# Other places and other lead for some loads of a retention-and-two-MLPs kernel: raw w_out, the joint products' weights, kept sums, activations

## The chip, the cores and the metric

The kernel runs on one core of one Trainium2 chip. The metric is device time in microseconds (us) of that core, from runs of the whole program; a second view is one profiled execution with its trace. Engines are called as in the profile: PE (matmuls), PEld (weight loads), DVE (vector), ACT (scalar), POOL, SP (a queue that here only issues DMAs).

## What is computed

Attention with a decay (no softmax) over 8 batches, 8 heads, 576 positions, head width 64; its output, 4608 tokens by 512, goes through two MLPs, 512 to 2048 to 512 each:

```python
ret = scores * Dmat[None]            # scores = q k^T / 8, Dmat = gamma**(i-j), lower triangle
x = matmul(ret, v)                   # -> 4608 x 512
h = x @ moe_w_in;   x = (h * sigmoid(1.702 * h)) @ moe_w_out
h = x @ moe2_w_in;  y = (h - tanh(h)) @ moe2_w_out
```

All of it is float32 to the outside. A product in the kernel is three passes over split operands (a high part rounded to fp32r and the remainder), `PASS` in the code.

## The kernel before

Tokens are cut into 9 blocks of 512, the inner dimension 2048 into 16 slices of 128. A "step" `n` of the first MLP is one slice of one block: `mm_in` (12 matmuls into one PSUM bank, L614), then `act_a` (a tanh on ACT, L628, and one operation on DVE, L630). Sixteen steps make a visit of a block. DVE and ACT run their instructions in the order in which the program gives them, and so does SP: a DMA whose buffer is not free yet holds up all DMAs behind it on SP. `h` has four PSUM banks, so PE can be some steps ahead of DVE.

**The sums.** The second product of the first MLP is done for visits 5 to 8 in pairs, by seven products of sums of quarters (a Winograd form) instead of eight. The operands of these products are formed while visits 6 and 8 run (`SUMMED`). Each odd step of such a visit calls `sums(u)` (L1206): two activations of this visit (`a21`, `a22`) and two of the visit before, which `firsts_load` (L1192) brought back from DRAM, give five results in four DVE operations (L1215 to L1218). The results go to DRAM by `stores` (L1180), named s1, s2 (in a place of `room`), s3 (the buffer of a21), s4 (the buffer of the loaded a12) and a22. `firsts_load` has three places, taken in turn, so a load for `u` waits for the store of s4 of `u - 3`.

**Raw w_out.** The weights of the same products are formed by `t_prep` (L964), a generator that is advanced by one piece per step: load two raw slices of w_out (tile `wr`, L990), two pairs of subtractions (L985), two splits into high part and remainder in `room` (L980, L981), two stores (`wt`, L971). Its tiles were the two of tag `gl`, so a pair is loaded one step ahead of its first subtraction.

**The joint products.** While the second MLP's first products run (`mm_part`, 6 matmuls each, L1042), the generator `out_units` is advanced in between; in its steps `k` of the joint kind a step is 12 matmuls (`mm_joint`, L741) on four accumulators: two pairs of blocks by two halves of the columns. There are seven stages of eight steps (`STAGES`). At the end of a stage each accumulator is emptied by `evac_joint` (L761); in five stages DVE adds a sum kept in DRAM (L774), which `kept_load` (L746) fetches at the start of the step with `q == 6`, that is one step ahead of the last. Two of the four tiles for it come from the rotation of six that `act_2` (L634) uses for its results (`turn("t")`). The step's weights come by `wj_load` (L276), in pairs, two steps ahead of the first; its activations by `g_load` (L702) into four places in turn, from which `act_b` (L713) splits them (L716 on ACT, L717 on DVE). Next to these, `wq_load` (L1005) fetches the second MLP's weights, two DMAs of 1 MB and 0.75 MB per `u`, and `g_store` (L655) stores its activations.

**The change of stages.** At step 141 of the first MLP (`n == NB * NF - 3`) the first weights and activations of the direct products of blocks 3 onward are loaded (`w_ahead`, `g_ahead`), and the first activation is split in the same step.

Of the kernel before, what the change touches and what calls it, by code (L numbers as in the profile page):

```python
# [8 lines left out]
F32 = mybir.dt.float32  # L9
# [8 lines left out]
P = 128  # L18
# [36 lines left out]
def kernel(  # L55
# [189 lines left out]
    def joint(k):  # L245
        return N1 <= k < N1 + NJ
# [25 lines left out]
        nc.sync.dma_start(out=t.rearrange("p a n -> p (a n)").bitcast(F32), in_=wo_d[int(j >= NB), f])  # L272

    wj = {}

    def wj_load(i):  # L276

        t = place(2 + i // 2 % 2)
        for n in range(2):
            stage, q = divmod(i + n, NF // 2)  # L280
            what, at_, h = STAGES[stage][1]
            src = wo_d[0, q + at_] if what == "o" else wt_d[q]
            c = ((0 if what == "o" else 2 * at_) + h) * DM
            nc.sync.dma_start(out=t[:, n].bitcast(F32), in_=src[:, c:c + DM])
            wj[i + n] = t[:, n].rearrange("p (a c) -> p a c", a=2)

    def wo_stay(f):

# [368 lines left out]
        nc.sync.dma_start(out=gd[s], in_=tt.pop(s))  # L657

    second = {}
    turns = {"t": 0, "gl": 0}  # L660

    def turn(what):

        shape, dt, n = {"t": ([P, BLK], F32, 3), "gl": ([P, BLK], F32, 2)}[what]
        i = turns[what]
        turns[what] += 1
        more = {"t": 3, "gl": 2}[what]
        if second and i % (n + more) >= n:
            return second["pool"].tile(shape, dt, tag=what + "2", name=what, bufs=more)
        return t_p.tile(shape, dt, tag=what, name=what, bufs=n)  # L670
# [12 lines left out]
    def joint_item(x):  # L683
        return N1 <= x < N1 + 2 * NJ
# [13 lines left out]
        return place(spot)  # L698

    def g_load(x):  # L700
        gl[x] = turn("gl")
        o = item(x)  # L702
        if joint_item(x):
            i, r = o
            stage, q = divmod(i, NF // 2)
            name = STAGES[stage][0]
            ja = ORDER[JOINT[r]]
            src = gd[ja * NF + q + (NF // 2 if name == "a12" else 0)] if name in ("a11", "a12") else gs[ja, name, q]
        else:
            src = gd.pop(step_of(o))  # L710
        nc.sync.dma_start(out=gl[x], in_=src)
# [34 lines left out]
    def kept_load(k):  # L746

        stage, q = divmod(k - N1, NF // 2)
        name = STAGES[stage][3]
        if name is None or q != NF // 2 - 2:  # L750
            return
        for y in range(4):
            r, m = divmod(y, 2)
            if y < 2:
                t = second["pool"].tile([P, BLK], F32, tag="o", name="kept", bufs=3)
            else:
                t = turn("t")
            nc.sync.dma_start(out=t, in_=kept_d[name, r, m])
            kept_t[y] = t
# [73 lines left out]
    def w_ahead(k):  # L833

        if not second:
            while n_w[0] <= min(k + 2, DIRECT * NF - 1):
                wo_load(n_w[0])
                n_w[0] += 1
            return
        if k == N1 - 2:  # L840
            wj_load(0)
        if joint(k) and (k - N1) % 2 == 0 and k + 2 < N1 + NJ:
            wj_load(k + 2 - N1)
        while n_w[0] <= min(k + 3, n_steps - 1):
            if joint(n_w[0]):
                n_w[0] = N1 + NJ
            elif n_w[0] == N1 + NJ and k < N1 + NJ - 2:
                break
            else:
                wo_load(n_w[0])  # L850
                n_w[0] += 1

    def g_ahead(x):

        while second and n_g[0] <= min(x + (7 if joint_item(x) else 4), n_b[0] + 3, n_items - 1):
            g_load(n_g[0])
            n_g[0] += 1
        while second and n_b[0] < n_items:
# [105 lines left out]
    def t_prep():  # L964
# [18 lines left out]

        h = slice(0, DM // 2), slice(DM // 2, DM)
        sub = lambda o, a, b: nc.vector.tensor_tensor(out=o, in0=a, in1=b, op=ALU.subtract)  # L985
        for q in range(NF // 2):
            wt_d[q] = dram.tile([P, 4 * DM], F32, tag=f"wt{q}", name="wt")
            lo, hi = ts = [t_p.tile([P, DM], F32, tag="gl", name="wr", bufs=2) for _ in range(2)]
            for i in range(2):
                nc.sync.dma_start(out=ts[i], in_=r_d[q + i * NF // 2])  # L990
            yield
            store()
            sub(lo[:, h[0]], lo[:, h[1]], lo[:, h[0]])
            sub(lo[:, h[1]], hi[:, h[1]], lo[:, h[1]])
            yield
# [3 lines left out]
            yield  # L999
            store()  # L1000
            halves_of(1, hi)
            yield
            store()

# [75 lines left out]
    def x2_std():  # L1080
        t = x_p.tile([P, KD, BLK], F32, tag="x", name="x2s")
        nc.sync.dma_start(out=t, in_=x2_d[0])
        yield
        xo["std"] = []
        for k in range(KD):
            xo["std"].append(xo_tile())
# [119 lines left out]
    def sums(u):  # L1206
# [9 lines left out]
        nc.vector.tensor_tensor(out=s2, in0=s1, in1=a11, op=ALU.subtract)  # L1216
        nc.vector.tensor_tensor(out=a12, in0=a12, in1=s2, op=ALU.subtract)
        nc.vector.tensor_tensor(out=a21, in0=a11, in1=a21, op=ALU.subtract)  # L1218
        done.extend(((j - 1, n, q), t) for n, t in (("a22", a22), ("s1", s1), ("s2", s2), ("s4", a12), ("s3", a21)))

    def some(it, n):
        for _ in range(n):
# [9 lines left out]
    for n in range(LAG, NB * NF):  # L1232
# [17 lines left out]
        if j in SUMMED:  # L1250
            u = SUMMED.index(j) * NF // 2 + f // 2
            if f % 2:
                sums(u)
                stores(5)
                if f < NF - 4:
                    firsts_load(u + 2)
            else:
                stores(2)
        else:
            if n >= LAG + DIRECT * NF:  # L1260
                done.append(s)
# [8 lines left out]
            spare = [x_p.tile([P, 2, 2, DM], F32R, tag="y", name="spare", bufs=2) for _ in range(2)]  # L1270
            room += [spare[i][:, k] for k in range(2) for i in range(2)]
        some(prep, 1)
        if n == NB * NF - 3:
            w_ahead(DIRECT * NF - 2)
            g_ahead(DIRECT * NF - 2)
        if j == NB - 1 and f >= 5:
            some(std, 1)
        if j == NB - 1 and f == 8:
            wq_load(0, True)
# [182 lines left out]
```

## Time and profile before

| | |
|---|---|
| median of 3 runs | 1758.8 us (1753.51 to 1760.52) |
| the profiled execution, its own time | 1754.56 us |
| its span, first to last instruction | 1752.8 us |
| mean granted PE clock | 0.980 |
| PE busy | 1663.6 us, 95% |
| DVE busy | 1225.8 us, 70% |
| ACT busy | 885.5 us, 51% |
| DMA moved | 510.6 MB, mean 291 GB/s |

PE is busy for 95% of the span, so the time is PE's work, plus the stretches in which PE waits, plus what PE loses where it is granted the half clock (0.50 in the tables below). The trace can be asked for who waited for whom, for the order of an engine's instructions in time, and for busy times by stretch. "DMA share" is the mean busy share of the 16 DMA engines.

### The profile page before, as it was taken

The numbers are of one execution on the slowest core, as the hardware profiler recorded it, in microseconds if no ns is written. First come the engines' busy times: TensorE is split into PE (matmuls) and PEld (weight loads), VectorE is DVE, ScalarE is ACT, GpSimd is POOL, SyncE is SP. The second block draws the span as 40 slices with busy tenths as digits, with TensorE's granted clock in tenths as the row PEclk, the third lists the DMA queues.
The fourth block names the chain that finished last, engine by engine and source line by source line (L and its number), as shares of the span: only waits on it lengthen the run. The fifth ranks groups of instructions, "written<-read, shape, count | busy, mean of one in ns | idle before, by whom it ended". The sixth has DMA issues, their size and how long they took to land.

```text
span 1752.8 us, 25320 instructions
## 1 busy us (share of the span) xinstructions
PE 1663.6 (95%) x8874; PEld 1348.8 (77%) x8874; DVE 1225.8 (70%) x1958; ACT 885.5 (51%) x1633; POOL 109.4 (6%) x99
## 2 busy tenths in 40 slices
PE   7999999999999698799999788889999999999999
PEld 5787888887888586588887666678888888888887
DVE  6787877878866657367687777666877777677542
ACT  5443443344432232356577566555776667666542
POOL 2111101221232000000000000000000000000000
PEclk8999999999999899899999899999999999999999
DMA  9566779889998878998898888889999988888962
GB/s 277 177 216 219 256 244 324 299 288 320 345 322 301 300 251 307 327 339 305 309 327 295 265 306 270 288 309 349 313 316 340 326 307 316 312 301 311 372 215 87
DMA packets 195504, 510.60 MB, mean 291 GB/s; under 512 B 21809, under 2 KB 31153, under 8 KB 186417
## 3 DMA queue, kind: packets, MB, share of 16 engines
q1 hardware_dynamic: 182704, 486.88, 80.0%
q10 hardware_dynamic: 12672, 22.11, 3.4%
q8 instruction: 70, 1.15, 0.3%
q14 instruction: 58, 0.47, 0.1%
HBM read 361.05 MB, written 147.85 MB: 290 GB/s over the span
## 4 chain that ended last, share of the span: by engine, by line
PE 70%; DMA 14%; DVE 9%; ACT 3%; issue 3%; SPq 2%; ACTq 0%; POOL 0%; DVEq 0%
PE acc L804 22%; PE h L614 13%; PE acc L800 12%; PE x L1042 8%; PE y L1042 4%; PE h L1029 2%; PE acc L741 2%; DMA gl<-gd 2%; PE w L1042 2%; DMA gl<-gs 2%; DMA wos<-wd 1%; DMA wr<-wr 1%; DVE t L630 1%; PE pat L536 1%; DMA gs<-t 1%
## 5 line engine op out<-in xcount | busy, mean ns | idle before, releaser
L614 PE MATMUL h<-xh,wi 128*128 128x512 f32 x1152 | 377.9, 398 | 22.9 <-DVE t L630 22.1
L804 PE MATMUL acc<-wos,g 128*128 128x512 f32 x1344 | 329.8, 390 | 5.3 <-DVE kept L774 5.3
L716 ACT ACTIVATE g<-gl 128x512 fp32r<-128x512 f32 x244 | 152.1, 628 | 304.0 <-PE acc L804 160.0
L804 PEld LDWEIGHTS acc<-wos,g 128*128 128x128 f32 x1344 | 252.9, 188 | 58.3 <-DVE kept L774 5.7
L717 DVE TENSOR_TENSOR g<-gl,g 128x512 fp32r<-128x512 f32 x244 | 166.6, 687 | 169.0 <-ACT g L716 167.4
L614 PEld LDWEIGHTS h<-xh,wi 128*128 128x128 f32 x1152 | 219.4, 190 | 76.8 <-DVE t L630 27.0
L614 PE MATMUL h<-xl,wi 128*128 128x512 f32 x576 | 227.4, 395 | 0.4 <-DVE xl L443 0.4
L1042 PE MATMUL x<-xo,wq 128*128 128x512 f32 x768 | 196.9, 392 | 0.0
L800 PE MATMUL acc<-g,wos 128*128 128x512 f32 x768 | 186.5, 392 | 1.4 <-DMA wos<-wd 1.1
L1042 PEld LDWEIGHTS x<-xo,wq 128*128 128x128 f32 x768 | 146.0, 190 | 30.9
L800 PEld LDWEIGHTS acc<-g,wos 128*128 128x128 f32 x768 | 142.8, 188 | 33.8 <-issue 2.7
L131 ACT ACTIVATE e<-e,ebias 128x512 int32<-128x512 int32 x64 | 46.4, 725 | 204.6 <-DVE e L129 199.2
L630 DVE SCALAR_TENSOR_TENSOR t<-t,h 128x512 f32<-128x512 f32 x144 | 97.5, 682 | 49.5 <-ACT t L628 49.4
L651 DVE SCALAR_TENSOR_TENSOR pl<-pl,sq 128x512 f32<-128x512 f32 x144 | 99.5, 691 | 42.3 <-ACT pl L648 40.2
L614 PEld LDWEIGHTS h<-xl,wi 128*128 128x128 f32 x576 | 109.8, 191 | 23.1 <-DVE xl L443 1.1
L741 PE MATMUL acc<-g,wos 128*128 128x512 f32 x408 | 106.1, 399 | 18.4 <-DVE kept L774 10.3
L653 DVE COPY_PREDICATED t<-marks,pl 128x512 f32<-128x512 int32 x144 | 109.5, 761 | 15.2 <-ACT g L716 0.5
L628 ACT ACTIVATE t<-h 128x512 f32<-128x512 f32 x144 | 83.1, 587 | 71.6 <-PE h L614 59.9
L741 PEld LDWEIGHTS acc<-g,wos 128*128 128x128 f32 x408 | 77.3, 192 | 38.3 <-issue 15.5
L648 ACT ACTIVATE pl<-sq,abias 128x512 f32<-128x512 f32 x144 | 104.3, 724 | 4.7
L649 ACT ACTIVATE marks<-sq,sbias 128x512 f32<-128x512 f32 x144 | 102.0, 709 | 0.0
L647 DVE TENSOR_TENSOR t<-h,t 128x512 f32<-128x512 f32 x112 | 76.9, 686 | 31.7 <-ACT t L644 17.1
(127 smaller groups left out, 2296.7 us busy)
## 6 DMA issues: line engine op xcount, KB each, us to landing
wos<-wd SPq DMA_DIRECT2D x176, 512.0 KB, 5.4
gd<-t SPq DMA_DIRECT2D x208, 256.0 KB, 5.0
gl<-gd SPq DMA_DIRECT2D x208, 256.0 KB, 5.2
wq<-wq SPq DMA_DIRECT2D x32, 1024.0 KB, 7.0
at<-in_attn_dram SPq DMA_DIRECT2D x29, 1024.0 KB, 6.5
stg<-in_w_dram SPq DMA_DIRECT2D x48, 512.0 KB, 6.4
wq<-wq SPq DMA_DIRECT2D x32, 768.0 KB, 8.5
gl<-gs SPq DMA_DIRECT2D x80, 256.0 KB, 4.7
```

Of the source, the lines that this page charges most:

```text
L614: nc.tensor.matmul(h, lhsT=win[f][:, a, k], rhs=xs[b][:, k], start=(n == 0), stop=(n == 3 * KD - 1))
L630: nc.vector.scalar_tensor_tensor(out=t, in0=t, scalar=1.0, in1=h, op0=ALU.add, op1=ALU.mult)
L648: nc.scalar.activation(out=pl, in_=sq, func=ACTF.Square, bias=abias)
L649: nc.scalar.activation(out=small, in_=sq, func=ACTF.Relu, bias=sbias, scale=-1.0)
L651: nc.vector.scalar_tensor_tensor(out=pl, in0=pl, scalar=CB, in1=sq, op0=ALU.add, op1=ALU.mult)
L653: nc.vector.copy_predicated(out=t, mask=small.bitcast(I32), data=pl)
L716: nc.scalar.activation(out=g[:, 0], in_=t, func=ACTF.Copy)
L717: nc.vector.tensor_tensor(out=g[:, 1], in0=t, in1=g[:, 0].bitcast(F32), op=ALU.subtract)
L741: nc.tensor.matmul(acc[y], lhsT=wo[:, a, m * P:(m + 1) * P], rhs=g[:, b], start=fresh and q == 0 and n == 0, stop=q == NF // 2 - 1 and n = ...
L800: nc.tensor.matmul(acc[m], lhsT=wh[:, m // 2, a, m % 2 * P:(m % 2 + 1) * P], rhs=g[:, b], start=first, stop=last)
L804: nc.tensor.matmul(acc[m], lhsT=g[:, a, c], rhs=wo[:, b], start=first, stop=last)
L1042: nc.tensor.matmul(ps, lhsT=wq[q][t][:, o // 2, o % 2 * 2 + k, a], rhs=xo[i][k][:, b], start=first and n == 0, stop=n == 5, skip_group_che ...
```

## The change

- `t_prep` loads raw w_out into three tiles of tag `stg`, one pair each, and two pairs ahead; a pair now takes three pieces instead of four.
- `firsts_load` is called in the even step, after the stores, instead of in the odd one; its condition changes with it. The results of `sums` are stored in another order, s4 first.
- `x2_std` (block 0 of the second MLP's input) is loaded two steps earlier and split one step later.
- The first loads of the direct products stand at step 138 instead of 141, the first split at 142.
- `wj_load` brings one operand per step, two steps ahead, into three halves of the same two tiles; the fourth half is a fifth place for `g_load`.
- `kept_load` stands one step earlier (`q` five instead of six).
- `g_ahead` may load one more item ahead among joint ones.

```diff
+    shared = []
     def wj_load(i):
-        t = place(2 + i // 2 % 2)
-        for n in range(2):
-            stage, q = divmod(i + n, NF // 2)
...
-            nc.sync.dma_start(out=t[:, n].bitcast(F32), in_=src[:, c:c + DM])
-            wj[i + n] = t[:, n].rearrange("p (a c) -> p a c", a=2)
+        if not shared:
+            shared.extend((place(3), place(2)))
+        t = shared[i % 3 // 2][:, i % 3 % 2]
+        stage, q = divmod(i, NF // 2)
...
+        nc.sync.dma_start(out=t.bitcast(F32), in_=src[:, c:c + DM])
+        wj[i] = t.rearrange("p (a c) -> p a c", a=2)
...
     def g_load(x):
-        gl[x] = turn("gl")
+        if x < N1:
+            spot = (x - DIRECT * NF) % 4 // 2
+        elif joint_item(x):
+            spot = (x - N1) % 5 // 2
+        else:
+            spot = 1 - (x - N1 - 2 * NJ) % 4 // 2
+        if spot == 0:
+            gl[x] = t_p.tile([P, BLK], F32, tag="gl", name="gl", bufs=2)
+        elif spot == 1:
+            gl[x] = second["pool"].tile([P, BLK], F32, tag="gl2", name="gl", bufs=2)
+        else:
+            gl[x] = shared[1][:, 1].bitcast(F32)
...
-        if name is None or q != NF // 2 - 2:
+        if name is None or q != NF // 2 - 3:
             return
...
-        if k == N1 - 2:
-            wj_load(0)
-        if joint(k) and (k - N1) % 2 == 0 and k + 2 < N1 + NJ:
+        if joint(k + 2):
             wj_load(k + 2 - N1)
...
-        while second and n_g[0] <= min(x + (7 if joint_item(x) else 4), n_b[0] + 3, n_items - 1):
+        while second and n_g[0] <= min(x + (7 if joint_item(x) else 4), n_b[0] + 3 + joint_item(x), n_items - 1):
...
+        def load(q):
+            t = raw[q] = st_p.tile([P, 2, DM], F32, tag="stg", name="wr", bufs=3)
+            for i in range(2):
+                nc.sync.dma_start(out=t[:, i], in_=r_d[q + i * NF // 2])
+
+        for q in range(2):
+            load(q)
+            yield
         for q in range(NF // 2):
             wt_d[q] = dram.tile([P, 4 * DM], F32, tag=f"wt{q}", name="wt")
-            lo, hi = ts = [t_p.tile([P, DM], F32, tag="gl", name="wr", bufs=2) for _ in range(2)]
-            for i in range(2):
-                nc.sync.dma_start(out=ts[i], in_=r_d[q + i * NF // 2])
-            yield
-            store()
+            t = raw.pop(q)
+            lo, hi = t[:, 0], t[:, 1]
...
             halves_of(1, hi)
+            if q + 2 < NF // 2:
+                load(q + 2)
             yield
...
-        yield
+        for _ in range(4):
+            yield
         xo["std"] = []
...
-        done.extend(((j - 1, n, q), t) for n, t in (("a22", a22), ("s1", s1), ("s2", s2), ("s4", a12), ("s3", a21)))
+        done.extend(((j - 1, n, q), t) for n, t in (("s4", a12), ("a22", a22), ("s1", s1), ("s2", s2), ("s3", a21)))
...
                 stores(5)
-                if f < NF - 4:
-                    firsts_load(u + 2)
             else:
                 stores(2)
+                if 0 < f < NF - 2:
+                    firsts_load(u + 1)
...
-        if n == NB * NF - 3:
+        if n == NB * NF - 6:
             w_ahead(DIRECT * NF - 2)
+            while n_g[0] < DIRECT * NF + 3:
+                g_load(n_g[0])
+                n_g[0] += 1
+        if n == NB * NF - 2:
             g_ahead(DIRECT * NF - 2)
-        if j == NB - 1 and f >= 5:
+        if j == NB - 1 and f >= 3:
             some(std, 1)
```

SP in visit 6, before. `a` are the tiles of `firsts_load`, `gs` its sums in DRAM, `wr` raw w_out; the store of `a_5257` is an s4, and the load into `a_5522` takes that tile's place:

```order
L1188 DMA gs<-t 128x512
L1188 DMA gs<-spare 128x512 x2
L919 DMA wq<-spare 128x1024
L1188 DMA gs<-a_5257 128x512
L1188 DMA gs<-t 128x512
L1203 DMA a_5522<-gd 128x512 x2
L990 DMA wr<-wr 128x512 x2
L1188 DMA gs<-t 128x512
```

The same place now; the load that takes the place of `a_5332` is the one into `a_5547`:

```order
L1206 DMA gs<-a_5332 128x512
L1206 DMA gs<-t 128x512
L1206 DMA gs<-spare 128x512
L1221 DMA a_5493<-gd 128x512
L1221 DMA a_5494<-gd 128x512
L929 DMA wq<-spare 128x1024
L1206 DMA gs<-spare 128x512
L1206 DMA gs<-t 128x512
L999 DMA wr<-wr 128x512 x2
L1206 DMA gs<-a_5389 128x512
L1206 DMA gs<-t 128x512
L1206 DMA gs<-spare 128x512
L1221 DMA a_5547<-gd 128x512 x2
L999 DMA wr<-wr 128x512 x2
```

Between the store of an s4 and the load that needs its place stood one DMA; now stand twelve, a whole pair of steps. The second of the two stores from `spare` (s2) has moved behind the load, one step later.

SP before, at the first load of kept sums in the joint products (`wq` the second MLP's weights, `wos<-wt` the step's weights, `gl` activations):

```order
L711 DMA gl<-gs 128x512 x2
L1019 DMA wq<-wq 128x2048
L1019 DMA wq<-wq 128x1536
L284 DMA wos<-wt 128x512 x2
L758 DMA kept<-kept 128x512 x2
L758 DMA t<-kept 128x512 x2
L711 DMA gl<-gs 128x512 x3
```

The same place now, where `wos<-gs` is the fifth place for activations:

```order
L286 DMA wos<-wt 128x512
L770 DMA kept<-kept 128x512 x2
L770 DMA t<-kept 128x512 x2
L723 DMA wos<-gs 128x512
L723 DMA gl<-gs 128x512
L1036 DMA wq<-wq 128x2048
L1036 DMA wq<-wq 128x1536
L286 DMA wos<-wt 128x512
L723 DMA gl<-gs 128x512 x2
L286 DMA wos<-wt 128x512
```

The kept sums now stand ahead of the large `wq` loads and not behind them, and the weights of the steps come one by one.

## Rows read from the trace of the kernel before

**Rows 1.** PE's waits, 556 to 732 us: waiter, releaser, us in total, times, longest.

```profile
PE h L614 <- DVE t L630: 22.1, 9, 7.4
PE h L1029 <- DVE t L630: 11.8, 1, 11.8
```

**Rows 2.** PE's waits, 870 to 1166 us, the same columns.

```profile
PE acc L741 <- DVE kept L774: 14.6, 3, 6.7
PE acc L741 <- DVE t L774: 7.6, 2, 4.6
PE acc L804 <- DVE kept L774: 5.3, 1, 5.3
PE acc L741 <- issue: 4.6, 3, 1.7
...
PE acc L741 <- DMA wos<-wd: 2.4, 1, 2.4
```

**Rows 3.** Half-clock stretches (columns as rows 4): five before 720 us, four after.

```profile
sum 34.13, PE 19.99 PEld 14.70 DVE 21.62 ACT 7.18 POOL 0.74; mean PE 4.00 PEld 2.94 DVE 4.32 ACT 1.44 POOL 0.15
...
978.73:992.38 13.65, 6.89 (x15) 4.81 (x16) 8.97 (x15) 6.17 (x11) 0.00 (x0) 0.50 0.95 329
...
1115.26:1122.09 6.83, 5.67 (x13) 4.32 (x14) 5.91 (x10) 3.52 (x6) 0.00 (x0) 0.50 0.82 285
...
sum 27.31, PE 19.02 PEld 14.17 DVE 19.06 ACT 12.06 POOL 0.00; mean PE 4.76 PEld 3.54 DVE 4.77 ACT 3.02 POOL 0.00
```

**Rows 4.** Stretches: length, busy PE, PEld, DVE, ACT, POOL, PE clock, DMA share, GB/s.

```profile
560.00:612.00 52.00, 38.61 (x313) 29.73 (x312) 27.21 (x51) 10.39 (x24) 5.84 (x5) 0.87 0.83 297
647.00:717.00 70.00, 49.75 (x196) 38.98 (x195) 41.70 (x69) 16.14 (x30) 0.00 (x0) 0.87 0.90 314
960.00:1165.00 205.00, 170.05 (x699) 135.63 (x698) 146.54 (x227) 117.35 (x205) 0.00 (x0) 0.93 0.84 289
1165.00:1400.00 235.00, 235.00 (x1038) 194.60 (x1037) 174.64 (x261) 153.15 (x267) 0.00 (x0) 1.00 0.92 323
1200.00:1250.00 50.00, 50.00 (x223) 41.39 (x222) 34.73 (x51) 30.85 (x54) 0.00 (x0) 1.00 0.98 362
1210.00:1220.00 10.00, 10.00 (x46) 8.29 (x45) 5.56 (x9) 3.65 (x7) 0.00 (x0) 1.00 1.01 406
```

**Rows 5.** Time order of SP, then DVE, visit 6: start us, us, instruction, [idle].

```profile
560.14 0.71 SPq L1188 DMA_DIRECT2D gs<-a  x1
...
569.05 0.79 SPq L1203 DMA_DIRECT2D a<-gd  x2
570.24 0.79 SPq L990 DMA_DIRECT2D wr<-wr  x2
...
575.30 0.42 DVE L985 TENSOR_TENSOR wr<-wr 128x256 f32<-128x256 f32 x1 [13.36 <-DMA wr<-wr]
```

**Rows 6.** Time order of SP, then ACT, at the end of visit 8.

```profile
706.35 0.47 SPq L711 DMA_DIRECT2D gl<-gd  x1
...
712.74 0.63 ACT L716 ACTIVATE g<-gl 128x512 fp32r<-128x512 f32 x1 [15.69 <-DMA gl<-gd]
```

**Rows 7.** Time order at two loads of the joint products: SP, DVE, SP, PE.

```profile
971.84 0.98 SPq L758 DMA_DIRECT2D kept<-kept  x2
...
981.12 0.69 DVE L774 SCALAR_TENSOR_TENSOR kept<-acc,kept 128x512 f32<-128x512 f32 x1 [7.41 <-DMA kept<-kept]
...
1039.86 1.16 SPq L284 DMA_DIRECT2D wos<-wd  x2
...
1047.48 0.70 PE L741 MATMUL acc<-wos 128*128 128x512 f32 x2 [2.37 <-DMA wos<-wd]
```

**Rows 8.** Time order at the end of a later stage: SP, ACT, PE.

```profile
1062.26 0.70 SPq L657 DMA_DIRECT2D gd<-t  x1
...
1068.60 0.60 ACT L644 ACTIVATE t<-x 128x512 f32<-128x512 f32 x1 [4.27 <-DMA gd<-t]
...
1073.94 1.36 PE L741 MATMUL acc<-wos 128*128 128x512 f32 x3 [4.65 <-DVE t L774]
```

More of the change, by code (lines that the diff above doesn't have):

```diff
@@ L274 @@
     wj = {}
+    shared = []
     def wj_load(i):
-        t = place(2 + i // 2 % 2)
-        for n in range(2):
-            stage, q = divmod(i + n, NF // 2)
-            what, at_, h = STAGES[stage][1]
-            src = wo_d[0, q + at_] if what == "o" else wt_d[q]
-            c = ((0 if what == "o" else 2 * at_) + h) * DM
-            nc.sync.dma_start(out=t[:, n].bitcast(F32), in_=src[:, c:c + DM])
-            wj[i + n] = t[:, n].rearrange("p (a c) -> p a c", a=2)
+        if not shared:
+            shared.extend((place(3), place(2)))
+        t = shared[i % 3 // 2][:, i % 3 % 2]
+        stage, q = divmod(i, NF // 2)
+        what, at_, h = STAGES[stage][1]
+        src = wo_d[0, q + at_] if what == "o" else wt_d[q]
+        c = ((0 if what == "o" else 2 * at_) + h) * DM
+        nc.sync.dma_start(out=t.bitcast(F32), in_=src[:, c:c + DM])
+        wj[i] = t.rearrange("p (a c) -> p a c", a=2)
     def wo_stay(f):
@@ L659 @@
     second = {}
-    turns = {"t": 0, "gl": 0}
+    turns = {"t": 0}
     def turn(what):
-        shape, dt, n = {"t": ([P, BLK], F32, 3), "gl": ([P, BLK], F32, 2)}[what]
+        shape, dt, n, more = {"t": ([P, BLK], F32, 3, 3)}[what]
         i = turns[what]
         turns[what] += 1
-        more = {"t": 3, "gl": 2}[what]
         if second and i % (n + more) >= n:
```

## Prediction

> **What bounds the kernel now.** I read the profile in this order: the waits of PE, the granted clock, the rates of the DMA engines by stretch, and then the time order of SP, DVE and ACT around each wait.
>
> PE is busy for 95% of the span, so what a change of loads can give back is PE's waiting. Between 556 and 732 us, which is visits 6 to 8 and the start of the second MLP, PE waits 22.1 + 11.8 = 33.9 us for DVE's L630 [rows 1]. In the joint products it waits 14.6 + 7.6 + 5.3 + 4.6 + 2.4 = 34.5 us [rows 2], mostly for DVE's L774. To each belongs a price in clock: in five stretches of the first part PE is granted the half clock (1.2 GHz of 2.4), in four of the second, and works 20.0 and 19.0 us in them [rows 3]. At the full clock that work takes half, so 10.0 and 9.5 us are lost. The two parts cost 43.9 and 44.0 us. The rest of the program the change leaves as it is.
>
> Neither DVE nor ACT is the origin. In visit 6 DVE stands idle for 13.36 us until raw w_out lands; that load was issued at 570.24, behind a load of `a` at 569.05, and this one had waited on SP for the store of s4 issued at 560.14 [rows 5]. So SP was held until its own store, 8.9 us old by then, had landed, the raw load came late, and it had one step (2.7 us: 12 matmuls at 50.00 us for 223 [rows 4]) of lead against 5.1 us of landing. At the end of visit 8 ACT idles 15.69 us until the first activation of the direct products lands, issued at 706.35 [rows 6]; the tanh of the last steps stands behind it on ACT. In the joint products the kept sums are issued at 971.84, behind 1.75 MB of `wq` in SP's order, and DVE gets them at 981.12 [rows 7], 9.3 us later.
>
> The resource behind it is the DMA engines. While PE waits they still move 297, 314 and 289 GB/s [rows 4]. The most that a stretch of 50 us shows is 362 GB/s, at a share of 0.98, and one of 10 us shows 406 [rows 4].
>
> **The sums and raw w_out.** No arithmetic is added or removed; the same DMAs, as many, move in order. Raw w_out now leads by four steps (two for the first pair), 10.9 us, against the 5.1 us of landing, in three tiles of its own; the load of `a` finds its s4 stored twelve DMAs earlier, so SP is held for two steps' worth less. The first activations of the direct products are issued four steps, 10.9 us, ahead of their split, against 712.74 - 706.35 = 6.4 us. With these the named causes of the 33.9 us and of the clock behind them go. What is late next is the DMA engines' pace. In 560 to 612 and 647 to 717, 122 us in all, they move 15.4 and 22.0 MB (length by rate), of which an estimate of 1.5 MB, raw w_out and what is formed of it, now goes between the two, since a pair takes three pieces. PE is busy for 38.61 + 49.75 = 88.4 us there and would need 10.0 less, 78.4 us [rows 3, 4]. At 362 GB/s 35.9 MB take 99.2 us. Stores may run over into what follows each stretch as far as buffers go, an estimate of 2.5 MB or 6.9 us each time, from a pair's seven DMAs of 256 KB and what lies between: 85.4 us. I take the middle, 92: a gain of 30 (23 to 44). The bytes that run over then meet the loads at the start of the second MLP; for that I take off 3 (0 to 6). **Sum of this part: 27 us, between 17 and 44.**
>
> An added wait is in it: s2 is now stored two steps after it is formed, and its place in `room` is next written one to two steps after that (2.7 to 5.4 us) where landing took 8.9 us at the worst [rows 5]. ACT or DVE would wait some 3 us at five or six such places in visit 6, with the tanh and so PE's `h` behind it; the four PSUM banks of `h` cover about three steps, 8 us, so I count it at nothing, and at 6 us where that cover is gone. The tiles of raw w_out were the decoder's; that has ended by then, so the tiles cost nothing. The later first split of `x2_std` (four steps of lead) and the order of the activations' places count at nothing, since their loads now land ahead.
>
> **The joint products.** Kept sums: from issue to the first emptying stood 21 matmuls in the order of PE, now 39, so 4.7 and 8.7 us at 0.224 us each; and the `wq` loads no longer stand ahead. The landing of 9.3 us behind `wq` is replaced by one like the 5.1 us of raw w_out [rows 5]. So the 14.6 us of waits for `kept`, a third of "issue", and the clock after them (half of 6.89 and of 5.67 us [rows 3]) go: 14.6 + 1.5 + 6.3 = 22.4 us.
>
> The other emptying waits have another cause, which the change leaves. At 1073.94 PE waits for `t` L774, DVE for ACT, and ACT at 1068.60 for a store of an activation issued at 1062.26 [rows 8]: two of the six tiles of `turn("t")` hold kept sums, so the tile that ACT needs belongs to a result whose store was issued one activation ago. The order of the tiles stays. Only the landing, 6.3 us, gets shorter, since 1 MB of kept sums no longer stands directly ahead of it: at 362 GB/s that is 2.8 us. Such waits are the 7.6, the 5.3 and two thirds of "issue", 3.1, with 3.2 us of clock: 19.2 us, of which I take back half, 9 (0 to 15).
>
> Weights singly: half of the operands had three steps of lead and now have two, 8.8 us (a step is 12 matmuls and its share of `mm_part`, 19.6 in all); landing was 7.6 us behind `wq` [rows 7]. The burst is halved, so between a gain of 2.7 and a loss of 6, I take nothing. The fifth place lets an activation's load be issued half a step earlier on SP, so loads and stores behind it too; within the 9 above.
>
> Again the pace: 960 to 1165 moves 205 x 289 = 59.2 MB; PE needs 170.05 - 9.5 = 160.5 us for it, at 362 GB/s the bytes take 163.6. That rate has been shown for 50 us only, so I take off 3 (0 to 10). **Sum: 22.4 + 9 - 3 = 28 us, between 12 and 38.**
>
> The Trainium skill bears on this pace: its page "DMA: Bandwidth & Descriptors", section "Where 436 GB/s comes from", says that for transfers between HBM and SBUF the HBM side binds, at about 358 GB/s for a core. The row of 10 us at 406 GB/s disagrees with it as a ceiling, the row of 50 us at 362 would pass for it. By that figure the two stretches of the sums would take 100.3 us together and the joint one 165.4, one to two us more than above.
>
> **The sum.** 1754.6 (the profiled execution) - 27 - 28 = 1699.6. The median of the runs shown is 4.2 us above that execution, the lowest 1.1 below it; I do not shift for it: **1700 us**.
>
> **The rivals.**
>
> *The DMA engines keep the pace that they held without waits of PE.* From 1165 to 1400 they moved 323 GB/s with PE never idle; only the 50 us at 362 within it lie higher for long [rows 4]. At that rate the stretches of the sums take 111 us together and the joint one 183; the gains are 11 and 22, together 33: 1722 us. For it: the shares of 0.83 to 0.90 in the stretches with waits. Against: the 362. (By the Trainium skill's page "DMA: Bandwidth & Descriptors", section "Where 436 GB/s comes from", such a ceiling exists, at a higher figure.)
>
> *All of it goes.* 43.9 + 44.0 with only the 10 us of `turn("t")` left: 1754.6 - 78 = 1676. It needs 35.9 MB in 78.4 us, 458 GB/s, which no row shows, unless more runs over than I estimate.
>
> *The sums' part does nothing.* SP is held at the load of `a` as before, because two steps are 5.4 us and a store took 8.9; raw w_out, at the back, still comes late. Then only the kept sums give, 22.4: 1732 us. Against: the DMAs behind s4 keep the engines filled while SP waits, which they did not before.
>
> *Slower: the weights of the steps.* Every operand now has two steps, 8.8 us. `wq` is loaded ten times in this part. If PE waited 2.4 us, as at 1047.48, for two operands behind each, with 1.7 us of half clock, that is 10 x 6.5 = 65 us; less the gains of 22.4 and 27 it ends at 1770 us. It decides from a landing above 8.8 us. The 7.6 measured is below that, with a pair of them in the burst.
>
> **How the numbers follow.** The forecast of 1700 has a chance of 0.52, 1722 has 0.22, 1676 has 0.12, the idle sums' part 0.06, slower 0.05, and 0.03 is no change at all by gains that are lost elsewhere. A measurement of this kernel can tell about 0.5%, 8.8 us, from no change. Of the 0.97, some of the tails of the middle cases come within that: faster 0.89, same 0.05, slower 0.06. The bounds of the terms give 1754.6 - 82 = 1673 to 1754.6 - 29 = 1726; the range takes in the third rival at 1732 and stops ahead of the slower one: 1674 to 1736.
>
> **What would show it.** Right, if PE's waits for L630 before 720 us fall from 33.9 to under 12 us, DVE's wait for raw w_out is gone, the wait for `kept` by DMA is gone, and the waits for L774 that stay follow an ACT wait for a store of an activation. DMA rates in the three stretches should rise to 340 to 370 GB/s. Wrong, if the rates stay near 320 with PE waiting for weights or for `h`; if DVE or ACT waits for stores from `spare`; or if PE's waits for the steps' weights grow beyond 6 us.

## The result and the profile after

The changed kernel takes 1705.1 us in the median of four runs (1696.9 to 1707.8) against 1757.7 for the kernel before (four runs): a ratio of 0.9695, 95% interval 0.9656 to 0.9733. The forecast was 1700, in a range of 1674 to 1736. The profiled execution took 1705.2 us, its span 1703.4 with a mean granted clock of 0.99; PE is busy for 97% of it, and the DMA engines move the same 510.6 MB at a mean of 300 GB/s.

PE's waits, from 540 to 732 us (first fence) and from there to 1166 us (second). Columns as in [rows 1]; L614, L630, L741, L774 and L804 of before are now L616, L632, L753, L786 and L816.

```profile
PE acc L812 <- DMA wos<-wd: 5.9, 1, 5.9
PE h L616 <- DVE t L632: 5.8, 2, 4.2
PE h L1046 <- DVE t L632: 0.9, 1, 0.9
```

```profile
PE acc L753 <- DVE t L786: 4.8, 4, 2.9
PE acc L816 <- DVE kept L786: 3.9, 1, 3.9
PE acc L753 <- issue: 3.7, 1, 3.7
PE acc L753 <- DMA wos<-wd: 3.4, 1, 3.4
PE acc L753 <- DVE kept L786: 2.1, 2, 1.2
```

Of the 33.9 us [rows 1] 5.8 + 0.9 = 6.7 are left, and a wait of 5.9 for weights of the second MLP's first products is new, or grown: one like it took 1.1 us before. In the joint products the waits of DVE's emptying [rows 2] fell from 27.5 to 10.8 us. The table of stretches, columns as in [rows 4], shows the half clock and the rates:

```profile
670.54:677.36 6.82, 4.67 (x11) 3.74 (x12) 3.97 (x6) 1.08 (x2) 0.00 (x0) 0.50 1.04 407
697.84:704.67 6.83, 6.10 (x14) 4.79 (x15) 3.13 (x5) 4.10 (x7) 0.00 (x0) 0.50 1.04 408
...
560.00:612.00 52.00, 50.45 (x435) 40.83 (x434) 41.35 (x77) 17.15 (x38) 5.50 (x5) 1.00 1.01 369
...
646.00:690.00 44.00, 38.89 (x162) 31.39 (x161) 30.48 (x47) 12.31 (x22) 0.00 (x0) 0.92 1.04 382
960.00:1165.00 205.00, 191.05 (x813) 154.73 (x812) 157.22 (x241) 128.96 (x224) 0.00 (x0) 0.98 0.89 312
...
924.00:1117.00 193.00, 177.12 (x749) 142.28 (x748) 155.04 (x240) 126.33 (x219) 0.00 (x0) 0.97 0.90 315
```

The last row is roughly the work that the kernel before did from 960 to 1165 us, since the same events lie some 25 to 50 us earlier now. At the half clock PE now works 4.67 + 6.10 us in the first part and 9.9 in three stretches of the second, against 19.99 and 19.02 [rows 3].

Where the time went is read best by laying the same event of both traces side by side, such as the tanh of one step or the emptying of one accumulator. At step 96 of the first MLP the kernel after is 0.9 us later; at the first tanh of the second MLP 35.4 us earlier; four steps on 27.7 earlier; at the last emptying of the joint products 49.8, and at the end 49.4. So the sums with the start of the second MLP gave 27.7 + 0.9 = 28.6 us, the joint products 49.4 - 27.7 = 21.7. The forecast had 27 and 28.

### The profile page after: what moved, and what is told of

The parts are those of the page before. It is cut to its first block, busy times and chain, and to the rows that moved or that the text cites. A ratio compares the mean times of both kernels' runs of the same rounds, so it can differ in the third digit from the quotient of the medians.

```text
span 1703.4 us, 25300 instructions
## 1 busy us (share of the span) xinstructions
PE 1651.0 (97%) x8874; PEld 1342.8 (79%) x8874; DVE 1228.3 (72%) x1958; ACT 886.6 (52%) x1633; POOL 110.6 (6%) x99
## 4 chain that ended last, share of the span: by engine, by line
PE 75%; DMA 12%; DVE 8%; ACT 2%; issue 2%; SPq 1%; ACTq 0%; DVEq 0%
PE acc L816 23%; PE h L616 14%; PE acc L812 12%; PE x L1059 8%; PE acc L753 5%; PE y L1059 4%; PE h L1046 2%; PE w L1059 2%; DMA gs<-spare 2%; DMA gs<-t 1%; DMA gl<-gs 1%; DMA wos<-wd 1%; PE pat L538 1%; DMA gl<-gd 1%; DVE t L632 1%
## 5 line engine op out<-in xcount | busy, mean ns | idle before, releaser
L616 PE MATMUL h<-xh,wi 128*128 128x512 f32 x1152 | 372.3, 394 | 6.6 <-DVE t L632 5.8
L816 PE MATMUL acc<-wos,g 128*128 128x512 f32 x1344 | 329.6, 390 | 4.0 <-DVE kept L786 3.9
L816 PEld LDWEIGHTS acc<-wos,g 128*128 128x128 f32 x1344 | 252.4, 188 | 57.4 <-DVE kept L786 4.4
L728 ACT ACTIVATE g<-gl 128x512 fp32r<-128x512 f32 x222 | 139.3, 628 | 268.1 <-PE acc L816 173.2
L616 PEld LDWEIGHTS h<-xh,wi 128*128 128x128 f32 x1152 | 217.3, 189 | 56.3 <-DVE t L632 7.1
L729 DVE TENSOR_TENSOR g<-gl,g 128x512 fp32r<-128x512 f32 x222 | 152.1, 686 | 147.0 <-ACT g L728 146.4
L616 PE MATMUL h<-xl,wi 128*128 128x512 f32 x576 | 225.4, 391 | 0.4 <-DVE xl L445 0.4
L632 DVE SCALAR_TENSOR_TENSOR t<-t,h 128x512 f32<-128x512 f32 x144 | 97.6, 682 | 54.4 <-ACT t L630 54.2
L630 ACT ACTIVATE t<-h 128x512 f32<-128x512 f32 x144 | 83.4, 587 | 85.1 <-PE h L616 59.9
L616 PEld LDWEIGHTS h<-xl,wi 128*128 128x128 f32 x576 | 108.7, 189 | 22.9 <-DVE xl L445 1.1
L753 PE MATMUL acc<-g,wos 128*128 128x512 f32 x408 | 104.9, 396 | 12.5 <-issue 3.7
L753 PEld LDWEIGHTS acc<-g,wos 128*128 128x128 f32 x408 | 77.2, 191 | 31.2 <-issue 13.0
L1059 PE MATMUL y<-xo,wq 128*128 128x512 f32 x384 | 99.3, 395 | 0.0
```

The lines of the kernel that those rows point to most:

```text
L616: nc.tensor.matmul(h, lhsT=win[f][:, a, k], rhs=xs[b][:, k], start=(n == 0), stop=(n == 3 * KD - 1))
L632: nc.vector.scalar_tensor_tensor(out=t, in0=t, scalar=1.0, in1=h, op0=ALU.add, op1=ALU.mult)
L728: nc.scalar.activation(out=g[:, 0], in_=t, func=ACTF.Copy)
L729: nc.vector.tensor_tensor(out=g[:, 1], in0=t, in1=g[:, 0].bitcast(F32), op=ALU.subtract)
L753: nc.tensor.matmul(acc[y], lhsT=wo[:, a, m * P:(m + 1) * P], rhs=g[:, b], start=fresh and q == 0 and n == 0, stop=q == NF // 2 - 1 and n = ...
L816: nc.tensor.matmul(acc[m], lhsT=g[:, a, c], rhs=wo[:, b], start=first, stop=last)
```

## The experiments

Each kernel below is the one after with a part undone, or something added. Times are medians, of four runs each, except the last with five; the kernel before took 1757.5 to 1758.8 beside them. The same event of two traces differs by up to 4 us ahead of any edit, so a part is read from the step between two events. Such a step, too, differs by 2 to 4 us between kernels that are the same there (from step 96 to the second MLP's fifth tanh by -2.3 to 3.4), and the four runs of the kernel after lie 11 us apart. So a part of 3 or 4 us is within the scatter.

### The joint part undone

`wj_load` in pairs, four places for `g_load`, `q != NF // 2 - 2` in `kept_load`, and no `joint_item(x)` in `g_ahead`, all as before.

> The kernel after with its joint products as before: weights in pairs, kept sums a step later, four places for activations. Lined up event by event, the two traces put 28.6 us of the 52.7 us down to the sums and the start of the second MLP, and 21.7 us to what follows. Theory A, the two parts are independent: 1757.7 - 28.6 = 1729 us, 1726 to 1732. Theory B, the sums' earlier loads are paid for in the joint products by bytes pushed into them, so that the joint part is worth more than 21.7 alone: above 1732. Theory C, the joint part gives less by itself, because the loads ahead of the joint products also gave some of it: below 1724.

Measured: 1728.2 us. That is theory A: the two parts are independent, and the joint one is worth 23 us.

### Kept sums one step later, and four places: which of the two gives it

```diff
-        if name is None or q != NF // 2 - 3:
+        if name is None or q != NF // 2 - 2:
```

> The kernel after with the kept sums loaded one step later, as before; all else as after. The prediction's term: 22.4 us come back, 1727 us (1720 to 1730), with DVE waiting for DMA of kept again. Rival: what the earlier load gave back was half hidden by the tiles' rotation, which holds PE at the same emptyings (waits of 2.9, 4.9 and 3.9 us stand there in the trace after): 8 to 12 us come back, 1713 to 1717.

Measured: 1711.1 us. Not 22, but 6 us come back (6.7 laid side by side), below the rival's 8 to 12.

```diff
-            spot = (x - N1) % 5 // 2
+            spot = (x - N1) % 4 // 2
...
-        while second and n_g[0] <= min(x + (7 if joint_item(x) else 4), n_b[0] + 3 + joint_item(x), n_items - 1):
+        while second and n_g[0] <= min(x + (7 if joint_item(x) else 4), n_b[0] + 3, n_items - 1):
```

> The kernel after with four places for the activations of the joint products in place of five, and their loads half a step later on SP. The prediction counted the fifth place within the 9 us of the emptyings: about 1705 us if it does nothing (1703 to 1708), up to 1714 if all that the emptyings gave came from it.

Measured: 1721.9 us, 17 us lost (16.1 side by side), more than either case allowed. The fifth place, with the load more that it allows ahead, was counted at next to nothing and is the larger part of the joint gain. The order of the two edits does not matter: from the kernel with the joint part undone, the early kept sums give 6.3 us with four places (1728.2 to 1721.9) and the fifth place 17.1 with late kept sums (1728.2 to 1711.1), each with the weights loaded singly. The two parts, 6.7 and 16.1, make the 23 of that kernel, so the weights give nothing that shows; they were not tried alone. What SP, the queue of the DMAs, waited for between 850 and 1120 us (columns as in [rows 1]) says more. In the kernel before:

```profile
SPq L711 <- DVE g L717: 64.7, 37, 4.7
SPq L711 <- DVE wos L717: 36.5, 21, 4.7
```

With four places:

```profile
SPq L723 <- DVE g L729: 53.6, 31, 4.9
SPq L723 <- DVE wos L729: 37.6, 20, 4.6
SPq L286 <- PE acc L753: 16.5, 20, 2.0
```

In the kernel after:

```profile
SPq L286 <- PE acc L753: 59.2, 36, 3.6
SPq L723 <- DVE g L729: 36.7, 23, 6.8
SPq L723 <- DVE wos L729: 12.6, 10, 2.9
```

L723 (L711 before) is the load of an activation, L729 (L717) the split that frees its place. With four places SP stands for 91 us at such a load, behind DVE, and the kernel before did the same for 101 us. Stores, weights and kept sums queue behind it. With five it waits rather for PE to free a place for weights (L286), which cost PE 3.4 + 0.7 us in all. SP does not stand less: it is 108 us over the three rows with four places and with five. What changed is for whom it stands. A wait for DVE closes a ring, since DVE's split waits for ACT, ACT for a load, and the load for SP; the ring is read from these rows and the next, and no run tests it by itself. ACT, from 850 to 1180 us, shows the other end. With four places:

```profile
ACT g L728 <- DMA gl<-gs: 32.7, 15, 5.1
ACT t L646 <- DMA gd<-t: 11.4, 6, 5.4
ACT g L728 <- DMA gl<-gd: 11.0, 5, 4.3
ACT wos L728 <- DMA gl<-gs: 6.1, 3, 3.2
ACT wos L728 <- DMA gl<-gd: 2.6, 3, 1.3
```

After:

```profile
ACT wos L728 <- DMA gl<-gs: 9.6, 5, 4.0
ACT t L646 <- DMA gd<-t: 7.5, 3, 4.6
ACT g L728 <- DMA gl<-gs: 7.3, 4, 2.3
ACT g L728 <- DMA gl<-gd: 6.8, 3, 3.8
ACT g L728 <- DMA wos<-gs: 6.4, 2, 5.1
```

The waits for loaded activations fall from 52.4 us to 32.4 (two rows of 1.6 and 0.7 are left out). The emptying hangs on that chain and not on the kept sums' landing. With four places they are loaded early and have landed 6.7 us before this emptying, and PE still waits 5.4 us for it; DVE, in order of time:

```profile
1037.10 0.69 DVE L729 TENSOR_TENSOR wos<-gl,wos 128x512 fp32r<-128x512 f32 x1 [2.33 <-ACT wos L728]
1038.36 0.69 DVE L649 TENSOR_TENSOR t<-h,t 128x512 f32<-128x512 f32 x1 [0.56 <-ACT t L646]
...
1042.37 1.28 DVE L786 SCALAR_TENSOR_TENSOR kept<-acc,kept 128x512 f32<-128x512 f32 x2
```

DVE reaches the emptying late, because the split and an activation stand ahead of it and wait for ACT. ACT starts at 1036.43, 0.1 us after the landing of its load (issued at 1030.20, landed at 1036.33); the profile names a matmul that ended in the same 0.1 us as the last that it waited for. With the kept sums late and five places DVE's wait for them is 1.8 us, against 12.1 in the kernel before and 12.9 with the joint part undone. In this order, from 845 to 1180 us:

```profile
DVE kept L786 <- DMA kept<-kept: 1.8, 1, 1.8
DVE kept L774 <- DMA kept<-kept: 12.1, 2, 7.4
DVE kept L784 <- DMA kept<-kept: 12.9, 3, 6.7
```

### Kept sums outside the rotation

Three kept sums in the tiles of the outputs, the fourth in a place of its own; that place comes out of the activations', which have four here (the edit of `g_load` for it is not shown).

```diff
-            if y < 2:
+            if y < 3:
                 t = second["pool"].tile([P, BLK], F32, tag="o", name="kept", bufs=3)
             else:
-                t = turn("t")
+                t = second["pool"].tile([P, BLK], F32, tag="k3", name="kept", bufs=1)
```

> The kernel after with four places for activations, and all four kept sums in tiles outside the rotation of the activations' tiles: three in the tiles of the outputs, one in a place of its own. Theory, the rotation: the tiles of two kept sums take two of the six that ACT's tanh turns through, so ACT waits for a store of an activation and PE for its emptying. PE's waits of 2.9, 4.9 and 3.9 us at the ends of three stages and 1.7 us of clock after each go: 1705.1 - 11.7 - 5.1 = 1688 us (1686 to 1694). Rival, these waits come from the landing of the kept sums or from DVE's own order, which the tiles don't change: 1702 to 1710, with the three waits still there, DVE waiting for DMA or for nothing.

Measured: 1711.7 us, 6.7 above the kernel after, so by the number the theory missed. But this kernel has four places for activations, and going from five to four cost 17 above, so against that kernel it is a gain of 10 (8 side by side). ACT's waits for the store of an activation (11.4 us with four places) are gone from the list; its waits for loaded activations are 57.8 us. The rotation was a cause, and it is worth 8 to 10 us, not the theory's 17; the fifth place is the better use of the same place.

### The sums, taken apart

```diff
-        for q in range(2):
-            load(q)
-            yield
+        load(0)
+        yield
+        yield
...
-            if q + 2 < NF // 2:
-                load(q + 2)
+            if q + 1 < NF // 2:
+                load(q + 1)
```

> The kernel after with raw w_out one pair ahead in place of two: each pair is loaded one step before its first use, as before, in the new tiles and the new order of stores. Theory A, the leads (the prediction): DVE idles for it again, some 3 us at each of eight pairs (5.1 to 6.5 us of landing against 2.7 of lead), with the tanh and PE behind it: 1714 to 1725 us. Theory B, the DMA engines' pace alone set the old time and the order of stores gave the gain: 1703 to 1709 us.

Measured: 1710.5 us, between the two cases; side by side 3.8 us are lost in the sums, hardly more than the scatter. DVE waits for raw w_out again, 15.4 us in all (first row; the second is the kernel before, both from 540 to 735 us), but PE pays little of it:

```profile
DVE wr L995 <- DMA wr<-wr: 15.4, 12, 5.3
DVE wr L985 <- DMA wr<-wr: 36.5, 15, 13.4
```

```diff
-        done.extend(((j - 1, n, q), t) for n, t in (("s4", a12), ("a22", a22), ("s1", s1), ("s2", s2), ("s3", a21)))
+        done.extend(((j - 1, n, q), t) for n, t in (("a22", a22), ("s1", s1), ("s2", s2), ("s4", a12), ("s3", a21)))
...
                 stores(5)
+                if f < NF - 4:
+                    firsts_load(u + 2)
             else:
                 stores(2)
-                if 0 < f < NF - 2:
-                    firsts_load(u + 1)
```

> The kernel after with s4 stored fourth of five, as before, and the loads of the activations for the sums two pairs ahead right behind the stores, as before. Theory A (the prediction): SP is held at the load of an activation until s4 has landed, two steps' worth of order; raw w_out, now two pairs ahead, does not suffer, but the stores behind do, and ACT's tanh waits for their tiles: 1710 to 1722 us. Theory B, with raw w_out early the hold costs nothing: 1703 to 1709 us.

Measured: 1723.9 us, 18.8 above; 15.9 side by side by the start of the second MLP. Theory A, by its upper end and beyond. SP's waits, 540 to 735 us: the load of an activation (L1221, before L1203) for the store of s4, here and in the kernel before.

```profile
SPq L1221 <- DMA gs<-a: 29.8, 6, 6.9
SPq L1203 <- DMA gs<-a: 29.2, 6, 7.0
```

The kernel after has no wait for that store at this line. SP in order of time, and the stretch in which it is held (columns as in [rows 4]):

```profile
573.57 0.38 SPq L1206 DMA_DIRECT2D gs<-t  x1
578.00 0.80 SPq L1221 DMA_DIRECT2D a<-gd  x2
```

```profile
575.00:578.00 3.00, 0.51 (x1) 0.50 (x2) 2.97 (x7) 2.43 (x7) 0.00 (x0) 0.80 0.68 262
```

For 4 us nothing is issued, and the DMA engines' share drops to 0.68 while more work waits behind the load. It reaches PE in two ways. In visit 6 the first pair of raw w_out stands behind a hold of 6 us, DVE idles 6.0 us for it, and PE waits 3.7 at 577.49. In visit 8, where raw w_out is done, ACT's tanh waits for a store of its tile, and PE 7.5 us at 685.99 and 1.9 after:

```profile
684.61 1.09 ACT L630 ACTIVATE t<-h 128x512 f32<-128x512 f32 x2 [10.20 <-DMA gs<-t]
```

DVE's waits for raw w_out come to 6.3 us here, where before they were 36.5, and still 15.9 of the 28.6 us are lost. So the hold costs that much with raw w_out early. How much more went through the late raw load in the kernel before, where both stood together, no run here tells: in this kernel it is 3.7 of the 14.0 us that PE waits for L632 in the sums.

```diff
-        if n == NB * NF - 6:
+        if n == NB * NF - 3:
             w_ahead(DIRECT * NF - 2)
-            while n_g[0] < DIRECT * NF + 3:
...
-        if n == NB * NF - 2:
             g_ahead(DIRECT * NF - 2)
```

> The kernel after with the first activations and weights of the second MLP's direct products loaded three steps before the end of visit 8, as before. Theory A (the prediction): the wait of 11.8 us and its 3.4 us of clock come back, as far as raw w_out didn't cause them: 1715 to 1721 us. Theory B, that load was late because SP was held by what is mended elsewhere, so its place in the order is worth little: 1703 to 1709 us.

Measured: 1708.2 us, theory B. PE's wait at the first tanh of the second MLP grows from 0.9 to 6.1 us, and the one for weights shrinks from 5.9 to 3.3: most of what the one loses the other gains. The three edits give 3.8, 15.9 and 0.8 us alone, 20.5 in all, of 28.6, and of these only the 15.9 is clear of the scatter. Where the other 8 come from stays open. They may show only where more than one edit is undone, which was not tried. And one part was never undone, the earlier load of `x2_std`. In the kernel before, ACT stood 12.3 us for it with the tanh behind, and PE 4.1 us behind that:

```profile
678.65 0.63 ACT L908 ACTIVATE xo<-x2s 128x512 fp32r<-128x512 f32 x1 [12.33 <-DMA x2s<-x]
680.65 0.50 PE L614 MATMUL h<-xh,wi 128*128 128x512 f32 x1 [4.09 <-DVE t L630]
```

In the kernel after ACT's wait for this load is 0.3 us.

### Is it the DMA engines' pace?

```diff
                 stores(5)
+                if f < NF - 6 or j != SUMMED[-1]:
+                    if 'x' not in firsts:
+                        firsts['x'] = place(2)
+                    nc.sync.dma_start(out=firsts['x'][:, f // 2 % 2].bitcast(F32), in_=gd[(j - 1) * NF + f])
```

> The kernel after with 13 more loads of 256 KB in visits 6 and 8 (8 and 5), of activations into a place that nobody reads: 3.4 MB. Theory, the DMA engines' pace sets the sums now: at 382 GB/s, the rate between 646 and 690 us, they cost 5.5 and 3.4 us, together 8.9: 1711 to 1716 us. Rival, there is slack in the buffers and the waits that remain come from the order: 0 to 3 us, 1704 to 1709.

Measured: 1711.3 us. By the start of the second MLP 9.8 us are lost, 8.9 were worked out from the rate; 2.8 of them come back within four steps and 2 in the joint products. The DMA engines' share is 1.02 from 560 to 612 us and 1.00 from 646 to 690, at 380 and 361 GB/s, so they stay full. A load more now costs the sums about what its bytes take. The loads also take turns on SP, which this run does not tell apart from their bytes.

```diff
-                nc.sync.dma_start(out=t[:, i], in_=r_d[q + i * NF // 2])
+                nc.gpsimd.dma_start(out=t[:, i], in_=r_d[q + i * NF // 2])
```

> The kernel after with the loads of raw w_out issued by GpSimd and not by SyncE; the bytes and their lead are the same. In the trace after, 33 of 56 of SP's DMAs between 560 and 612 us and 44 of 76 between 647 and 720 were issued at the very moment at which the DMA eight before them had landed, so SP seems to have eight in flight at most. Theory A, that number sets the pace of the sums: two loads a pair less in it, so PE's waits of 4.2 and 0.9 us near 680 us and their clock shrink: 3 to 8 us less, 1697 to 1702. Theory B, the DMA engines are full (a share of 1.02 to 1.05 at 370 to 395 GB/s in these stretches), and eight in flight is only how the queue looks from SP: 1703 to 1708. GpSimd may take longer to issue than SP: then the raw loads come late and it is 1708 to 1715, with DVE waiting for wr.

Measured: 1706.4 us, but no run lies there: two took 1702 us, two 1710 to 1711. The median speaks for theory B, the runs for the edge of A and for the third case, so the number decides nothing. The trace, of a run of 1702, does not either. All sixteen loads were issued by 612 us, so SP had none fewer near 680, where theory A has its waits; they are 3.4 and 2.0 us, after 4.2 and 0.9. In visit 6, where SP was relieved, PE never waits from 560 to 596 us. But it does not wait there either in the first kernel above, whose sums are those of the kernel after (first row; the second is this run):

```profile
560.00:596.00 36.00, 36.00 (x324) 29.40 (x323) 31.97 (x54) 11.63 (x26) 5.59 (x5) 1.00 1.03 393
560.00:596.00 36.00, 36.00 (x324) 29.42 (x323) 31.60 (x55) 13.55 (x31) 9.34 (x13) 1.00 1.04 397
```

So no gain of this edit is shown, and whether the number in flight costs anything near 680 us stays open.

### The start of the second MLP, and one kept sum fewer

Ahead of `for q in (1, 2): wq_load(q, True)`; the second edit is `y < 3` in `kept_load`, with `turn("t")` for the fourth.

```diff
+    while n_w[0] < DIRECT * NF + 4:
+        wo_load(n_w[0])
+        n_w[0] += 1
     for q in (1, 2):
```

> The kernel after with two edits that lie 200 us apart, so that the trace tells them apart: at the start of the second MLP the next two operands of w_out are loaded ahead of four loads of wq (0.5 MB each) and not behind them; in the joint products three of four kept sums lie in the tiles of the outputs, so that one and not two takes a tile out of the activations' rotation. Theory, queue behind wq: PE's wait of 5.9 us at 698.57 us goes, with up to 3 us of clock, so the first emptying of the joint products comes 6 to 9 us earlier; rival, the landing is set by the bytes in flight whatever their order, and wq's own operands come late in turn: 0 to 2. Theory, rotation: ACT's 7.5 us of waits for stores of activations halve, and of PE's 16.5 us of waits at the emptyings a third goes with its clock: 4 to 8 us more; rival, the emptyings wait for the loads of activations: 0 to 2. Both theories together 1688 to 1695, both rivals 1701 to 1706 us.

Measured: 1696.8 us (1695.3 to 1699.6), a ratio to the kernel before of 0.9655 (0.9638 to 0.9671), 8 us below the median of the kernel after, of whose four runs one, 1696.9, was as fast. Laid side by side, 3.0 us came at the start of the second MLP and 5 in the joint products, most of it at their last emptying, where PE's wait of 3.9 is down to 0.8. The rotation's theory holds; the two kernels below, with the same kept sums, show 4.9 and 4.2 us in the joint products. At the start it is half of the theory, and no more than the scatter: the wait for weights is gone, and the next load behind `wq` takes its place.

```profile
PE acc L812 <- ACT g L728: 3.4, 1, 3.4
```

```profile
698.97 1.28 ACT L728 ACTIVATE g<-gl 128x512 fp32r<-128x512 f32 x2 [13.76 <-DMA gl<-gd]
```

Two edits aim at that load. The first issues `wq` after the steps' own loads, `wq_load(i + 1, True)` in the first two steps; the second issues one activation more ahead of `wq`.

> The kernel with w_out's operands first and one kept sum in the rotation, and the two later loads of wq at the start of the second MLP moved behind the first and second emission of its steps, so that the first loads of activations, too, stand ahead of them on SP. Theory: the first activation, issued at 689.38 us behind 2 MB of wq and landed at 698.86, lands near 693; PE's wait of 3.4 us and the half clock after it (3.4 us of loss) go: 1696.8 - 5 = 1692 us (1689 to 1694). Rival, wq is late in its turn at the second and fourth step: 1697 to 1704.

Measured: 1700.9 us, the rival. `wq` itself is late now, and after it the activation's own operations on DVE:

```profile
697.83 3.00 PE L1046 MATMUL h<-xo,wq 128*128 128x512 f32 x12 [1.47 <-DMA wq<-wq]
715.15 1.22 PE L1046 MATMUL h<-xo,wq 128*128 128x512 f32 x2 [3.44 <-DVE pl L654]
```

> The kernel with w_out's operands first and one kept sum in the rotation, and one load of an activation more ahead of the four loads of wq; these are 0.7 us later for it, and the next loads come in the same order. Theory: the activation that ACT got at 698.86 us, 9.5 us after its issue, lands near 692; PE's wait of 3.4 us at 699.65 and its half clock go: 1696.8 - 4 = 1693 us (1690 to 1695). Rival: wq's first pair, wanted at about 696 us, is late by as much, or the next activation takes the place of this one: 1696 to 1700.

Measured: 1695.6 us (1693.4 to 1701.1), not to be told from 1696.8. The wait of 3.4 us is gone, and one of 2.1 for the next weights, issued at 690.15 and landed at 701.13, stands in its place. Three orders were tried there, and in each another load came late.

## Why the prediction was right or wrong

**The time and the sign** hold, 1705 for 1700. The two parts came close as well, but not each by its own steps: errors of opposite sign cancel in both, so the closeness is in part luck.

**The sums, 27: measured 28.6.** The gain was 36.3 and not 30, within 23 to 44; what was given back was 7.7 and not 3, beyond the bound of 6. The mis-sized term is mostly the pace. The prediction took 362 GB/s as the most that a stretch of 50 us showed; the trace of before has one of 368 (columns as in [rows 4]):

```profile
766.00:816.00 50.00, 50.00 (x222) 41.42 (x221) 34.39 (x50) 29.13 (x51) 0.00 (x0) 1.00 0.99 368
```

The kernel after holds 382 for 44 us. At that rate the 35.9 MB would take 94.0 us and not 99.2, an estimate, which is up to 5.2 of the 6.3 us. So more went through in the sums, and a wait of 5.9 us with 3 of half clock met the start of the second MLP. (The Trainium skill, "DMA: Bandwidth & Descriptors", section "Where 436 GB/s comes from", puts the HBM side at about 358 GB/s for a core; the rows of 382 over 44 us and 397 over 36 disagree with it as a ceiling.) That bytes set the pace is borne out by the extra loads, 9.8 us for 8.9. Of the causes, SP held by s4 was named and is the main one that the runs show, 15.9 us. The prediction made raw w_out the link from it to the tanh in visit 6; the run with s4 late shows the loss with raw w_out two pairs ahead. There its first pair is one link, 3.7 us of PE's waits, and a late store of the tanh's tile a larger one, 7.5. The load of `x2_std` was counted at nothing, but PE's 4.1 us behind it were among the 33.9.

**The added wait for s2, counted at nothing:** it came, and with it one of the signs of being wrong, waits of ACT for stores from `spare`. From 540 to 735 us they are 24.1 us in five places, the longest for a store of formed weights (`wt`); in the kernel before 4.3 us, once, were for a sum:

```profile
  DMA gs<-spare: 14.2, 4
  DMA wt<-spare: 9.9, 1
```

PE's only wait near them is 1.55 us, at 588.72. So the sign misled, and the cover that was named, the banks of `h`, held.

**Kept sums, 22.4: measured 6.7.** The failed step is the reading of "DVE waits for `kept`" [rows 7] as the origin. That wait was the last of a chain that ran late anyhow: SP stood at a load for which no place was free, and the kept sums, the activations' loads and the stores all queued behind it. With five places the wait falls to 1.8 us although the kept sums are loaded as late as before. **The fifth place, counted within 9: measured 16.1.** The same chain, in which a place more turns SP's wait for DVE into one for PE. The prediction saw that it lets a load go half a step earlier, and stores behind it; it didn't ask how long SP was held there and for whom, though 101 us behind DVE stood in the trace of before. **The tiles of `turn("t")`** are a cause, as [rows 8] had it: their full removal gave 8 to 10 us with four places, and one tile less 4 to 5 with five. **Weights singly: nothing** that shows, as predicted; PE's waits for them are 3.4 + 0.7 us, under the 6 that were named as a sign. **The sum of 28, measured 21.7,** is nearer than its terms: one is 15.7 us too high, another more than 7 too low.

**The rivals.** Of the rates forecast at 340 to 370 GB/s, the two of the sums came (369 from 560 to 612 us, 348 from 647 to 717), the one of the joint products did not: 312 from 960 to 1165 us, 315 for the same work, near the 323 of the first rival. But PE waits there more for DVE's emptying, 10.8 us, than for weights, 4.1, and the DMA engines' share is 0.90, where the sums have 1.01 to 1.04. So the rival's cause, bytes, is not borne out. All of it going, the idle sums and the slower weights are excluded.

## What to carry over

On a queue that issues in order, add up how long it stands at each line, for whom, and what lies behind. A buffer more at the load where SP stood longest for DVE, and a store issued earlier where SP stood for its landing, were worth 16 us here each. The loads that looked late behind them gave 4 to 7 us when undone alone. The length of the wait does not say it: with the fifth place SP stands as long as with four, but for PE. The engine that waits last for a DMA names a symptom; undo one edit at a time before believing it, and undo all of them, since the one left out may hold the rest. Where bytes filled the engines, at the start of the second MLP, moving a load ahead of another mostly moved the wait.

## What the runs showed of the hardware

In none of these traces were more than eight of SP's DMAs in flight at once, the one being issued counted. In the kernel after, 33 of its 56 issues between 560 and 612 us and 44 of 76 between 647 and 720 came at the moment the eighth DMA before had landed; in the kernel before 2 of 42 and 5 of 75. With sixteen loads on GpSimd's queue up to 12 were in flight over both queues between 540 and 612 us, and the rate from 560 to 596 was 397 GB/s, against 393 with all on SP. So in that stretch the number in flight was a sign of full engines and hardly a limit; for the stretch near 680 us no run tells.

From 672 to 682 us the kernel after moves 403 GB/s; a DMA of 256 KB lands each 0.64 us between 677 and 685, 5.0 to 6.5 us after its issue. The rates of 382 GB/s over 44 us and 397 over 36, at shares of 1.04, are above the best that the trace of before shows for so long, 373 from 1205 to 1249 us and 380 from 1623 to 1659.
